# A soft mixture of experts behind windowed attention: k and v of a batch loaded in rows of 36 tokens on every other partition, and expert 6's w2 all in column slabs

## The chip, the cores and the metric

The kernel runs on one core of one Trainium2 chip. The metric is the time of one execution in device microseconds; lower is better. Four runs of the kernel before took 177.62 to 177.84 us, with a median of 177.7 us.

## The reference

The inputs are q, k and v of shape (8 batches, 8 heads, 576 tokens, 64) and the weights phi (512, 32), w1 (8, 512, 1024) and w2 (8, 1024, 512), all float32.

```
scores = q @ k.T / 8            # per batch and head
# heads 0-3: token i sees j with 0 <= i-j < 32
# heads 4-7: token i sees j with 0 <= i-j < 128 and (i-j) % 4 == 0
attn = softmax(where(mask, scores, -1e9)) @ v
x = attn as (4608 tokens, 512)
logits = x @ phi                                # 32 slots, 4 for each of 8 experts
slot_input = softmax(logits, over tokens).T @ x
slot_out[e] = relu(slot_input[e] @ w1[e]) @ w2[e]
out = softmax(logits, over slots) @ slot_out    # (4608, 512)
```

## The kernel before

**Tiling.** The attention is cut into 16 halves: half i is batch i // 2, with the first four heads (the plain window) if i is even and the last four (the window with steps of 4) if it is odd. `half(i)` (line 476) writes down all operations of a half. q, k and v of a half come from memory in three transfers (`load_half`, line 330), each with 128 rows: partition 32*h + p holds 18 consecutive tokens of head h, so a row is 18 x 64 values, 4608 bytes read and 2304 written, since the transfer turns float32 into bf16. The staging area has NSTG = 4 places, so it holds four halves. VectorE turns each staged tensor in blocks of 32 x 32 words (a word is a pair of bf16 values) into the layout that the matmuls read, with the pairs of the head dimension on partitions (`turn`, lines 485 to 497; one instruction of 576 words, or four short ones at line 494 for q of an odd half). The turned tensors stand in `o_kqv`, two places of one half each.

After that a half runs through scores with the mask added by a matmul (lines 509 to 533, TensorE), exponentials (548, ScalarE), v turned by TensorE and copied (570, 576), the product with v (603, 627), division by the row sum (610, 614, 635, 638, VectorE) and a turn of x (654 to 677). An odd half then adds the logits (693), their exponentials (701) and the slot inputs (730, 735, 743) of its batch.

**The experts.** All weights are kept in SBUF as bf16. w1 takes 2 MB of reading per expert and w2 as much. `w2off` (line 314) puts w2 of experts 0 to 4 into an area of their own and w2 of experts 5 to 7 over the staging area, so the loads of the latter have to wait until the last staged tensor has been turned (`rd` at lines 390 to 392). Most weights are loaded whole, in rows of 8192 written bytes (`w1_piece`, `w2_piece`). The last part of w2 comes in column slabs (`w2_slab`): first columns 0 to 255 of all remaining rows, then columns 256 to 511, in rows of 512 written bytes. Before the change the slabs hold the second half of expert 6's rows and all of expert 7's, 1.5 MB of reading for each slab, in pieces of 4, 4, 2, 1 and 1 rows for each partition; the first half of expert 6 is loaded whole, as a transfer of 4 rows for each partition.

**The end.** Behind the attention come the two layers of the experts (`L1` at 818, `L2` at 857), which read the weights in the order in which they land. When the first slab is in, columns 0 to 255 of the slot outputs are complete (881), and the output tiles of those columns are computed (901), scaled (910 on ScalarE, 913 on VectorE) and stored (922) for the first five half groups of tokens (NA = 2.5). When the second slab is in, the other columns of those, and then all other groups in whole rows, follow. The output is 9.4 MB in float32.

**What sets the order.** The kernel does not leave its order to a compiler. Each operation is written down with its engine, a duration that was put in by hand and a priority from `OFFS` and `PERIOD`; `Sched.run` (line 121) plays this through and gives each engine's order, and semaphore waits are added where an operation needs another engine's result. The loads of q, k, v and of all weights but one (half of expert 0's w1, on SyncE's queue) are issued by GpSimd on one queue, q0, in an order written out by hand: lines 779 to 786 put the three loads of half i, then `W_AFTER[i]` weight pieces, then those of half i + 1. A load that has to wait on GpSimd holds up all behind it. The stores are issued by SyncE on another queue.

Of the kernel before, what the change touches and what calls it, by code (L numbers as in the profile page):

```python
# [12 lines left out]
B, H, S, D = 8, 8, 576, 64  # L13
# [5 lines left out]
NH = 16  # L19


W_AFTER = [0, 1, 1, 0, 1, 0, 1, 0, 1, 0, 1, 0, 1, 0, 0, 99]
PERIOD = 22.6
NSTG = 4
PE_SLOW = 1.1
LRU = 130.0

OFFS = dict(T=64.4, SC=177.5, EX=-17.6, MK=58.6, TB=-42.6, VE=-89.4, PV=-21.2, RC=-6.8,
            NM=-229.1, XT=-20.7, XE=15.1, LG=-37.0, EXL=132.1, ET=25.9, EE=0.6, SI=26.7, SA=50.4)


class Buf:
# [164 lines left out]
def bass_dilated_sliding_attn__then__soft_moe_slots_kernel(  # L197
# [15 lines left out]
    def take(n):  # L213
        o = top[0]
        top[0] = o + (n + 1) // 2 * 2
        return o

    o_w1 = take(8 * 4 * FF)
    o_w2 = take(5 * 8 * DM)
    o_stg = take(max(NSTG * 3 * 1152, 3 * 8 * DM))  # L220
    o_kqv = [take(3 * 1152) for _ in range(2)]
    NP = 4
    PW = 4 * 320 + 64
    o_p = [take(PW) for _ in range(NP)]
# [33 lines left out]
    def a(off, dims, p0=0, pn=128):  # L258
        return AP(ar, p0 * NBF + off, [[NBF, pn]] + dims)
# [4 lines left out]
    def af(off, dims, p0=0, pn=128):  # L264
        return AP(ar_f.tensor, (p0 * NBF + off) // 2, [[NBF // 2, pn]] + dims)
# [22 lines left out]
    def dvet(n, psum=False):  # L288
# [1 line left out]

    b_id, b_mp, b_md, b_oh, b_sel, b_rm, b_phst, b_phis = (Buf(n) for n in
        ("id", "mp", "md", "oh", "sel", "rm", "phst", "phis"))
    b_stg = [[Buf(f"stg{i}{j}") for j in range(3)] for i in range(NSTG)]
    b_kqv = [[Buf(f"kqv{i}{j}") for j in range(3)] for i in range(2)]
    b_p = [Buf(f"p{i}") for i in range(NP)]
    b_vb = [[Buf(f"vb{i}{j}") for j in range(2)] for i in range(NVB)]
    b_xp = [Buf(f"xp{i}") for i in range(NX)]
# [8 lines left out]
    b_w1 = [Buf(f"w1{e}") for e in range(8)]  # L306
    b_w2 = [[Buf(f"w2{e}{s}") for s in range(2)] for e in range(8)]
    b_sx = Buf("sx")
    b_w6h = Buf("w6h")
    b_w2h = [[Buf(f"w2h{x}{s}") for s in range(2)] for x in range(4)]  # L310
    b_htz, b_rt, b_so = Buf("htz"), Buf("rt"), [Buf("soA"), Buf("soB")]
    b_hsb = [Buf(f"hsb{x}") for x in range(2)]
# [5 lines left out]
    def sem(n):  # L318
        return [nc.alloc_semaphore(n), 0]

    s_stg = [[sem(f"s_in{i}{j}") for j in range(3)] for i in range(NSTG)]
    loads = {}

    def dma_in(fn, nbytes, s, prio, name, **kw):
# [2 lines left out]
        loads[name] = o  # L327
        return o

    def load_half(i):  # L330
        b, dl = i // 2, i % 2
        s = i % NSTG
        for j, src in ((1, k), (0, q), (2, v)):
            def fn(src=src, j=j, s=s, b=b, dl=dl):
                return pool.dma_start(  # L335
                    a(o_stg + (s * 3 + j) * 1152, [[1, 1152]]),
                    src[b, 4 * dl:4 * dl + 4].rearrange("h (p t) d -> (h p) (t d)", p=32))
            dma_in(fn, 128 * 1152 * 4, s_stg[s][j], (-100.0 if i < 2 else -80.0) + i, f"ld{i}{'qkv'[j]}",
                   writes=[b_stg[s][j]])

    wq = []
    shared = {}
# [20 lines left out]
    def w2_piece(e, c0=0, n=8):  # L363
        def fn():
            return pool.dma_start(
                a(w2off(e) + c0 * DM, [[1, n * DM]]),
                moe_w2[e].rearrange("(p c) f -> p (c f)", c=8)[:, c0 * DM:(c0 + n) * DM])
        return (fn, n << 18, f"w2_{e}{c0}", b_w2[e] if e < 6 else [b_w6h])

    def w2_slab(e, s, c0=0, n=8):  # L370
        def fn():
            return pool.dma_start(  # L372
                a(w2off(e) + 256 * s + c0 * DM, [[DM, n], [1, 256]]),
                moe_w2[e].rearrange("(p c) f -> p c f", c=8)[:, c0:c0 + n, 256 * s:256 * s + 256])
        return (fn, n << 17, f"w2s_{e}{s}{c0}", [b_w2[e][s] if e == 6 else b_w2h[(0, 4, 6, 7).index(c0)][s]])

    wq += [w1_piece(e, 2 if e == 0 else 0) for e in range(8)]
    wq += [w2_piece(e) for e in range(6)] + [w2_piece(6, 0, 4)]
    for s in range(2):
        wq += [w2_slab(6, s, 4, 4), w2_slab(7, s, 0, 4), w2_slab(7, s, 4, 2),  # L380
               w2_slab(7, s, 6, 1), w2_slab(7, s, 7, 1)]
    nw = [0]

    def load_w(n):
        for _ in range(n):
            if nw[0] >= len(wq):
                return
            fn, nb, name, wr = wq[nw[0]]
            e = int(name.split("_")[1][0])
            rd = []  # L390
            if name.startswith("w2") and e >= 5:
                rd = [x for y in b_stg for x in y]
            nw[0] += 1
            dma_in(fn, nb, w_sem(name), rate=384e3 if name[2] == "s" else 422e3,
                   lag=(2.9 if name[2] == "s" else 2.3) if name[:2] == "w2" else 0.8, prio= -100.0 if nw[0] < 2 else -80.0, name=name, writes=list(wr) + rd)


    op(SP, lambda: spq.dma_start(
        af(w2off(4), [[1, 2048]]),
        w1_rows(0)[:, :2048]), .1, -200.0,  # L400
       kind="dma", nbytes=1 << 20, sem=sem("s_w1f"), writes=b_w2[4], name="w1f")
    for x in range(2):
        op(ACT, lambda x=x: act.activation(
            a(o_w1 + 1024 * x, [[1, 1024]]), af(w2off(4) + 2048 * x, [[1, 1024]]), ACTF.Copy),
            1.1, -200.0, reads=b_w2[4], writes=[b_w1[0]], name=f"w1c{x}")


    def const_ops():
# [67 lines left out]
    def half(i):  # L476
        b, dl = i // 2, i % 2
        T0 = i * PERIOD
        st, kq = i % NSTG, i % 2
        pr = lambda s: T0 + OFFS[s]  # L480
        ok, oq, ov = (o_kqv[kq] + 1152 * j for j in range(3))
        bq, bk, bv = b_kqv[kq][0], b_kqv[kq][1], b_kqv[kq][2]
        oq, ok = ok, oq

        def turn(j, o_dst):
            src = o_stg + (st * 3 + j) * 1152
            if not (dl and j == 0):
                return dve.transpose(au(o_dst, [[1, 18], [18, 32]]), au(src, [[32, 18], [1, 32]]))  # L488
            for x in range(4):

                na = (18 - x + 3) // 4
                t0, t1 = x, 18 + x
                at = [(t % 4) * 144 + t // 4 for t in (t0, t1)]
                last = dve.transpose(  # L494
                    au(o_dst + 2 * at[0], [[1, na], [9, 16], [at[1] - at[0], 2]]),
                    au(src + 64 * x, [[128, na], [1, 32]]))
            return last

        for j, o_dst in ((1, ok), (0, oq), (2, ov)):
            first_t.append(op(  # L500
                DVE, lambda j=j, o_dst=o_dst: turn(j, o_dst),
                1.43 if dl and j == 0 else 1.24, pr("T") + (0.5 if j == 2 else 0.0),
                reads=[b_stg[st][j]], writes=[b_kqv[kq][j]], name=f"T{i}{'qkv'[j]}"))

        def sc_fn(r):
            last = None
# [262 lines left out]

    last_ex = [None]  # L770
    for i in range(NH):
        load_half(i)
        half(i)
        if i == 0:
            load_phi(first_t[0])
        if i in (9, 13):
            row_sums(0 if i == 9 else 3, 3 if i == 9 else 6, 15 * PERIOD)
    names = [w[2] for w in wq]
    load_w(99)
    dma_order, w_at = [], 0  # L780
    for i in range(NH):
        dma_order += [f"ld{i}{c}" for c in "kqv"]
        dma_order += names[w_at:w_at + W_AFTER[i]]
        w_at += W_AFTER[i]
    for x, y in zip(dma_order, dma_order[1:]):
        loads[y].ord = loads[x]
    assert len(dma_order) == len(loads)
# [63 lines left out]
    def l2(es, x, col, n, cs=range(8), bufs=None):  # L851
        def fn():
            last = None
            for c in cs:
                for e in es:
                    g, j = e // 4, e % 4
                    last = pe.matmul(pf(sobank[x].idx, 0, [[1, n]], 32 * j, 32),  # L857
                                     a(o_htz + 1024 * g + 128 * c + 32 * j, [[1, 32]]),
                                     a(w2off(e) + DM * c + col, [[1, n]]),
                                     start=(c == 0 and g == 0 or x > 0 and c == (4 if e == 6 else 0)),  # L860
                                     stop=(c == (3 if e == 6 and x == 0 else 7) and (x > 0 or e in (3, 4, 5, 6))))
            return last

        op(PE, fn, pet(len(cs), n * .92), T1 + 5 + 2 * es[0] + (20 if x == 2 else 0) + cs[0] / 8,
           reads=[b_htz] + (bufs or [b_w2[e][y] for e in es for y in range(2)]),
           rmw=[sobank[x]], name=f"L2{es[0]}{x}{cs[0]}")

    l2((0, 1, 2, 3), 0, 0, 512)
    l2((4,), 0, 0, 512)
    l2((5,), 0, 0, 512)  # L870
    l2((6,), 0, 0, 512, range(4), [b_w6h])
    op(ACT, lambda: act.activation(a(o_so, [[1, 512]], 0, 64), pf(sobank[0].idx, 0, [[1, 512]], 0, 64),
                                   ACTF.Copy), actt(512), T1 + 10, reads=[sobank[0]], writes=b_so,
       name="SOx")
    op(DVE, lambda: dve.tensor_copy(af(o_sx, [[1, 512]], 64, 64), pf(sobank[0].idx, 0, [[1, 512]], 64, 64)),
       dvet(512, True), T1 + 10, reads=[sobank[0]], writes=[b_sx, b_p[2]], name="SOy")
    for x in (1, 2):
        l2((6,), x, 256 * x - 256, 256, range(4, 8), [b_w2[6][x - 1]])
        for y, cs in enumerate((range(4), range(4, 6), range(6, 7), range(7, 8))):
            l2((7,), x, 256 * x - 256, 256, cs, [b_w2h[y][x - 1]])  # L880
        op(DVE, lambda x=x: dve.tensor_tensor(  # L881
            a(o_so + 256 * x - 256, [[1, 256]], 64, 64), pf(sobank[x].idx, 0, [[1, 256]], 64, 64),
            af(o_sx + 512 * x - 512, [[1, 256]], 64, 64), AluOp.add), dvet(256, True),
           T1 + 10 + 20 * x, reads=[sobank[x], b_sx], writes=[b_so[x - 1]], name=f"SO{x - 1}")
# [139 lines left out]
```

## Time and profile before

| | |
|---|---|
| median of 4 runs | 177.7 us |
| the profiled execution | 177.78 us |
| its span in the profile | 176.0 us |
| TensorE, matmuls busy | 123.7 us (70% of the span) |
| VectorE busy | 121.0 us (69%) |
| ScalarE busy | 104.4 us (59%) |
| GpSimd busy | 44.6 us (25%) |
| read from memory, written to it | 61.93 MB, 9.44 MB, 406 GB/s over the span |

The page of the profile gives, after such totals, the span in 40 equal slices of 4.4 us. A digit there is the busy share of an engine in tenths; the row DMA is the mean busy share of the 16 DMA engines, and GB/s is what they moved, counted in written bytes. Then come the DMA queues with their packets and bytes (a packet is one row as one engine moves it), and the issues of transfers with the median time from issue to landing. A timeline lists instructions in order of time as start, duration, engine, line, operation and tiles; in brackets stands how long the engine was idle before and what ended that. PE is TensorE's matmuls, PEld its weight loads, DVE VectorE, ACT ScalarE, POOL GpSimd and SP SyncE. The profile's span is shorter than the time of the execution by 1.78 us.

### The profile page before, as it was taken

The page shows a single profiled execution, that of the slowest core. Times are in us where ns is not written, and L with a number is a line of the kernel's source. Part 1 is how long each engine was busy: PE and PEld are TensorE (multiplying, and loading weights), DVE is VectorE, ACT ScalarE, POOL GpSimd, SP SyncE. Part 2 cuts the span into 40 slices and gives each one's busy share as a digit, 9 for nine tenths or more (in the row PEclk, how much of TensorE's full clock was granted, in tenths as well). Part 3 has the DMA queues.
Part 4 walks back from the last instruction along what each step waited for, and adds up shares of the span by engine and source line. Part 5 has one row for each costly group of instructions (what it writes and reads, how often), then busy time and mean ns, then how long its engine had stood idle before and what let it go on. Part 6 is the DMA issues. An engine that isn't in the chain of part 4 may idle for free.

```text
span 176.0 us, 4779 instructions
## 1 busy us (share of the span) xinstructions
PE 123.7 (70%) x2098; PEld 83.5 (47%) x2098; DVE 121.0 (69%) x218; ACT 104.4 (59%) x165; POOL 44.6 (25%) x90
## 2 busy tenths in 40 slices
PE   0008767798899989889698889996776566897000
PEld 0005545676567667567477467775433123431000
DVE  6899589698988997995997899757220002699200
ACT  2404498697889789689489668884411001499000
POOL 7659632132412321420550000394000000000000
PEclk9999999999999999999999999999999999999655
DMA  5999999999999999999999999999999999999997
GB/s 171 243 210 210 221 204 214 219 208 208 219 211 208 222 208 209 221 210 204 216 216 210 207 216 219 216 214 220 212 216 216 209 194 189 281 330 413 419 425 318
DMA packets 16469, 41.26 MB, mean 234 GB/s; under 512 B 1729, under 2 KB 7361, under 8 KB 13889
## 3 DMA queue, kind: packets, MB, share of 16 engines
q0 software_dynamic: 12304, 30.41, 89.4%
q1 hardware_dynamic: 4144, 10.55, 15.9%
q8 instruction: 16, 0.26, 0.5%
q14 instruction: 5, 0.03, 0.0%
HBM read 61.93 MB, written 9.44 MB: 406 GB/s over the span
## 4 chain that ended last, share of the span: by engine, by line
DMA 47%; DVE 22%; PE 11%; ACT 6%; POOL 4%; issue 2%; POOLq 0%; DVEq 0%
DMA ar<-in_v_dram 29%; DMA ar<-in_moe_w_dram 18%; DVE ar L488 7%; DVE ar L913 6%; ACT ar L548 3%; PE ps L509 3%; POOL ar L372 3%; DVE ar L614 2%; PE ps L603 2%; DVE ar L444 2%; PE ps L570 1%; PE ps L516 1%; DVE ar L449 1%; DVE ar L494 1%; ACT ar L670 1%
## 5 line engine op out<-in xcount | busy, mean ns | idle before, releaser
L488 DVE STREAM_TRANSPOSE ar<-ar 128x576 uint32<-128x576 uint32 x40 | 48.8, 1242 | 5.2 <-DMA ar<-in_k_dram 3.7
L548 ACT ACTIVATE ar<-ps 128x1152 bf16<-128x1152 f32 (+1 forms) x32 | 38.0, 1186 | 24.2 <-PE ps L533 15.0
L509 PE MATMUL ps<-ar 128*128 128x320 bf16 (+1 forms) x128 | 22.7, 301 | 18.2 <-DVE ar L488 13.7
L614 DVE TENSOR_TENSOR ar<-ps,fs 96x768 bf16<-96x768 f32 (+1 forms) x32 | 26.3, 822 | 1.2
L576 ACT ACTIVATE ar<-ps 128x768 bf16<-128x768 bf16 x32 | 25.0, 812 | 1.1 <-PE ps L570 1.0
L509 PEld LDWEIGHTS ps<-ar 128*128 128x128 bf16 x128 | 10.4, 99 | 23.2 <-DVE ar L488 13.7
L603 PE MATMUL ps<-ar 128*128 128x65 bf16 x320 | 14.7, 193 | 4.5 <-ACT ar L548 3.9
L570 PE MATMUL ps<-ar 128*128 128x128 bf16 x192 | 15.8, 228 | 1.9 <-DVE ar L614 1.0
L335 POOL DMA_DIRECT2D ar<-in_k_dram x16 | 8.8, 553 | 28.1 <-DVE ar L488 25.0
L603 PEld LDWEIGHTS ps<-ar 128*128 128x128 bf16 x320 | 12.0, 97 | 7.5 <-ACT ar L548 4.5
L910 ACT ACTIVATE ar<-ps,fs 128x512 f32<-128x512 f32 (+1 forms) x23 | 11.4, 638 | 5.7 <-PE ps L901 5.7
L857 PE MATMUL ps<-ar 128*32 128x512 bf16 (+1 forms) x76 | 10.8, 347 | 5.3 <-DMA ar<-in_moe_w_dram 4.6
L570 PEld LDWEIGHTS ps<-ar 128*128 128x128 bf16 x192 | 12.4, 118 | 3.2 <-DVE ar L614 1.5
L913 DVE TENSOR_SCALAR ar<-ps,fs 128x512 f32<-128x512 f32 (+1 forms) x23 | 12.7, 625 | 1.0 <-PE ps L901 1.0
L335 POOL DMA_DIRECT2D ar<-in_v_dram x16 | 8.8, 547 | 13.6 <-DVE ar L488 10.3
L610 DVE RECIPROCAL fs<-ps 96x12 f32<-96x12 f32 (+1 forms) x32 | 6.5, 202 | 7.7 <-PE ps L603 7.2
L901 PE MATMUL ps<-ar 128*128 128x512 bf16 (+1 forms) x46 | 9.9, 340 | 1.3 <-DVE ar L881 1.0
L335 POOL DMA_DIRECT2D ar<-in_q_dram x16 | 8.7, 544 | 7.9 <-DVE fs L610 4.2
L670 ACT ACTIVATE ar<-ps 128x576 bf16<-128x576 bf16 x16 | 9.7, 659 | 0.9 <-PE ps L654 0.7
L693 PE MATMUL ps<-ar 128*128 128x288 bf16 x64 | 9.2, 287 | 1.2 <-ACT ar L677 1.2
L857 PEld LDWEIGHTS ps<-ar 128*32 128x32 bf16 x76 | 4.5, 96 | 11.6 <-DMA ar<-in_moe_w_dram 8.4
L673 ACT ACTIVATE ar<-ps 128x1024 bf16<-128x1024 bf16 x8 | 8.2, 1030 | 2.5 <-PE ps L660 2.3
(75 smaller groups left out, 181.1 us busy)
## 6 DMA issues: line engine op xcount, KB each, us to landing
ar<-in_moe_w_dram POOLq DMA_DIRECT2D x13, 1024.0 KB, 28.2
out_dram<-ar SPq DMA_DIRECT2D x6, 1024.0 KB, 8.6
ar<-in_k_dram POOLq DMA_DIRECT2D x16, 288.0 KB, 22.7
ar<-in_q_dram POOLq DMA_DIRECT2D x16, 288.0 KB, 23.3
ar<-in_v_dram POOLq DMA_DIRECT2D x16, 288.0 KB, 22.9
out_dram<-ar SPq DMA_DIRECT2D x10, 256.0 KB, 3.1
ar<-in_moe_w_dram SPq DMA_DIRECT2D x1, 1024.0 KB, 5.1
ar<-in_moe_w_dram POOLq DMA_DIRECT2D x2, 512.0 KB, 21.4
```

The lines of the kernel that those rows point to most:

```text
L335: return pool.dma_start(a(o_stg + (s * 3 + j) * 1152, [[1, 1152]]), src[b, 4 * dl:4 * dl + 4].rearrange("h (p t) d -> (h p) (t d)", p=32))
L488: return dve.transpose(au(o_dst, [[1, 18], [18, 32]]), au(src, [[32, 18], [1, 32]]))
L509: pe.matmul(pf(h, 0, [[1, W]]), a(o_id, [[1, 128]]), a(msk, [[1, W]]), start=True, stop=False)
L548: eo = op(ACT, lambda P=P, W=W: act.activation(a(P, [[W, 4], [1, W]]), AP(ps, 0, [[4096, 128], [512, 4], [1, W]]), ACTF.Exp, scale=SCALE), ...
L570: last = pe.transpose(pb(bank.idx, bb * 256 + par * 32, [[64, 4], [1, 32]]), src, a(o_id, [[1, 128]]))
L576: op(ACT, lambda t=t, bank=bank: act.activation(a(o_vb[vs] + 3 * t * VBK, [[66, 12], [2, 32], [1, 2]]), pb(bank.idx, 0, [[64, 12], [1, 32] ...
L603: last = pe.matmul(pf(bank.idx + x, 65 * t, [[1, 65]]), w, a(VB + t * VBK + 66 * h, [[1, 65]]), start=True, stop=True)
L614: op(DVE, lambda hp=hp, bank=bank: dve.tensor_tensor(a(ox + 128 * hp, [[64, 2], [256, NT], [1, 64]], 0, rows), pf(bank.idx, 0, [[512, 2], ...
L670: fn = lambda c=c + x, bank=bank: act.activation(a(o_xt[xt] + 576 * c, [[1, 576]]), pb(bank.idx, 0, [[1, 576]]), ACTF.Copy)
L857: last = pe.matmul(pf(sobank[x].idx, 0, [[1, n]], 32 * j, 32), a(o_htz + 1024 * g + 128 * c + 32 * j, [[1, 32]]), a(w2off(e) + DM * c + co ...
L910: op(ACT, lambda: act.activation(dst, src(), ACTF.Copy, scale=sca), actt(cw, .1), prio + .1, reads=[bank, b_rinv], writes=wr, name=f"OE{G} ...
L913: op(DVE, lambda: dve.tensor_scalar(dst, src(), sca, None, op0=AluOp.mult), dvet(cw, True) + .08, prio + .1, reads=[bank, b_rinv], writes= ...
```

## The change

Three things are changed together, and the planner's priorities (`OFFS`, `PERIOD`) are other numbers.

For batches 1 to 7, k and v are loaded in rows of 36 tokens. One transfer takes four heads: 64 rows of 9216 bytes read and 4608 written. The first four heads go to the even partitions, the last four to the odd ones. A block of 32 partitions then holds one head of the first four and one of the last four, and two VectorE instructions for each tensor turn the whole batch, for both halves together. q, and all of batch 0, are loaded and turned as before. The staging area holds NSTG = 2 batches in place of four halves, with the same bytes; a k or v load waits until both instructions that turn this tensor of the batch two before are done. The turned tensors need twice the room: one of the two places is put over w2 of expert 3 and a part of expert 4's, whose loads now wait for the last use of what stands there.

The weights between the batches are one piece fewer: six w1 pieces come before the last batch's loads, and seven did. The first megabyte of expert 0's w1 is staged in the place of expert 0's w2, where it was expert 4's.

The half of expert 6's w2 rows that was loaded whole goes back into the slabs, which so hold all of experts 6 and 7, 2 MB of reading each. Expert 5's w2 is loaded in two halves of 4 rows for each partition in place of one transfer, and each half has matmuls of its own.

```diff
-W_AFTER = [0, 1, 1, 0, 1, 0, 1, 0, 1, 0, 1, 0, 1, 0, 0, 99]
-PERIOD = 22.6
-NSTG = 4
+W_AFTER = [1, 0, 1, 1, 1, 1, 1, 99]
+PERIOD = 8.7
+NSTG = 2
+LOADS = (((1, 0), (0, 0), (2, 0), (1, 1), (0, 1), (2, 1)), ((1, 0), (1, 1), (0, 0), (2, 0), (2, 1), (0, 1)))
...
-    o_stg = take(max(NSTG * 3 * 1152, 3 * 8 * DM))
-    o_kqv = [take(3 * 1152) for _ in range(2)]
+    o_stg = take(max(NSTG * 3 * 2304, 3 * 8 * DM))
+    o_kqv = [o_w2 + 3 * 8 * DM, take(3 * 2304)]
...
+    def load_batch(b):
+        s = b % NSTG
+        for j, x in LOADS[b > 0]:
+            def fn(j=j, x=x, src=(q, k, v)[j][b, 4 * x:4 * x + 4]):
+                o = o_stg + (s * 3 + j) * 2304
+                if j == 0 or b == 0:
+                    return pool.dma_start(a(o + 1152 * x, [[1, 1152]]),
+                                          src.rearrange("h (p t) d -> (h p) (t d)", p=32))
+                return pool.dma_start(AP(ar, x * NBF + o, [[2 * NBF, 64], [1, 2304]]),
+                                      src.rearrange("h (u t) d -> (h u) (t d)", u=16))
+            dma_in(fn, 128 * 1152 * 4, s_stg[s][j][x], (-100.0 if b < 1 else -80.0) + 2 * b,
+                   f"ld{b}{'qkv'[j]}{x}", writes=[b_stg[s][j][x]] if j == 0 or b == 0 else b_stg[s][j])
...
-    wq += [w2_piece(e) for e in range(6)] + [w2_piece(6, 0, 4)]
+    wq += [w2_piece(e) for e in range(5)] + [w2_piece(5, 0, 4), w2_piece(5, 4, 4)]
     for s in range(2):
-        wq += [w2_slab(6, s, 4, 4), w2_slab(7, s, 0, 4), w2_slab(7, s, 4, 2),
+        wq += [w2_slab(6, s), w2_slab(7, s, 0, 4), w2_slab(7, s, 4, 2),
                w2_slab(7, s, 6, 1), w2_slab(7, s, 7, 1)]
...
+        def turn(j, x):
+            src = o_stg + (st * 3 + j) * 2304
+            return dve.transpose(au(o_kqv[kq] + 2304 * j + 36 * x, [[1, 18], [36, 16], [576, 2]]),
+                                 au(src + 64 * 18 * x, [[32, 18], [1, 32]]))
...
+        for j in (1, 0, 2):
+            if j == 0 or b == 0:
+                first_t.append(op(
+                    DVE, lambda j=j: turn_half(j), 1.43 if dl and j == 0 else 1.24,
...
+            elif not dl:
+                for x in range(2):
+                    op(DVE, lambda j=j, x=x: turn(j, x), 1.24, pr("TK" if j == 1 else "TV") + .05 * x,
+                       reads=b_stg[st][j], writes=b_kqv[kq][j], name=f"T{b}{'qkv'[j]}{x}")
...
-    l2((5,), 0, 0, 512)
-    l2((6,), 0, 0, 512, range(4), [b_w6h])
+    for y in range(2):
+        l2((5,), 0, 0, 512, range(4 * y, 4 * y + 4), [b_w5h[y]])
...
     for x in (1, 2):
-        l2((6,), x, 256 * x - 256, 256, range(4, 8), [b_w2[6][x - 1]])
+        l2((6,), x, 256 * x - 256, 256, bufs=[b_w2[6][x - 1]])
```

## The prediction

> **What bounds the kernel now.** I read the 40 slices first, then the queues, then stretches of the DMA record, and last the weight loads of TensorE at the end.
>
> ```profile
> PE   0008767798899989889698889996776566897000
> DVE  6899589698988997995997899757220002699200
> DMA  5999999999999999999999999999999999999997
> GB/s 171 243 210 210 221 204 214 219 208 208 219 211 208 222 208 209 221 210 204 216 216 210 207 216 219 216 214 220 212 216 216 209 194 189 281 330 413 419 425 318
> q0 software_dynamic: 12304, 30.41, 89.4%
> ```
>
> No compute engine is full over the span, and DVE is nearly idle after slice 28. The DMA row is 9 from the second slice to the last but one. GB/s counts what is written: on q0 each bf16 byte written is two fp32 bytes read, so 210 there is 420 read. The transfers set the end; anything that does not change how long the 16 DMA engines need, or when the last load is in, is free.
>
> ```profile
> ar<-in_k_dram POOLq DMA_DIRECT2D x16, 288.0 KB, 22.7
> ar<-in_q_dram POOLq DMA_DIRECT2D x16, 288.0 KB, 23.3
> ar<-in_v_dram POOLq DMA_DIRECT2D x16, 288.0 KB, 22.9
> ```
>
> A q, k or v load lands 23 us after its issue in the median, though one takes about 1.4 us: the queue has some 20 us of work in front of each. That is the cover for every wait on POOL.
>
> Now the price of a row. Each stretch below holds q0 packets of one size: 2304 B (q, k, v) from 94 to 104 us, 8192 B (whole weight rows) from 108 to 138, 512 B (column slabs) from 144.5 to 148.5. The packets under 512 B are the completion marks, one per engine and transfer.
>
> ```profile
> DMA packets 1014, 2.11 MB, mean 211 GB/s; under 512 B 112, under 2 KB 112, under 8 KB 1012
> q0 software_dynamic: 1012, 2.07, 109.8%
> ...
> q0 software_dynamic: 878, 6.41, 102.4%
> ...
> DMA packets 1594, 0.78 MB, mean 194 GB/s; under 512 B 79, under 2 KB 1594, under 8 KB 1594
> q0 software_dynamic: 1594, 0.78, 144.6%
> ```
>
> One packet of one engine therefore takes 10 us x 16 / (1012 - 112) = 177.8 ns at 2304 B; 30 us x 16 / (878 - 96) = 613.8 ns at 8192 B (96 marks there); 4 us x 16 / (1594 - 79) = 42.2 ns at 512 B. A line through the outer two is 4.1 ns per packet plus 0.0744 ns per byte. It gives 175.6 ns at 2304 B, 2.2 below the measured, and 347.1 ns at 4608 B. Packets overlap (the shares are over 100%), so the mean duration of one record (192 ns at 2304 B, 60 ns at 512 B) is not its price: those would give a fixed 22 ns per packet, five times too much.
>
> Last, the loads of the column stage, each seen by the matmuls that wait for it:
>
> ```profile
> 141.51 1.41 PEld L857 LDWEIGHTS ps<-ar 128*32 128x32 bf16 x8 [3.34 <-DMA ar<-in_moe_w_dram]
> 143.96 0.54 PEld L857 LDWEIGHTS ps<-ar 128*32 128x32 bf16 x4 [1.05 <-DMA ar<-in_moe_w_dram]
> 145.31 0.33 PEld L857 LDWEIGHTS ps<-ar 128*32 128x32 bf16 x4 [0.80 <-DMA ar<-in_moe_w_dram]
> 146.69 0.33 PEld L857 LDWEIGHTS ps<-ar 128*32 128x32 bf16 x4 [1.06 <-DMA ar<-in_moe_w_dram]
> 147.33 0.11 PEld L857 LDWEIGHTS ps<-ar 128*32 128x32 bf16 x2 [0.31 <-DMA ar<-in_moe_w_dram]
> 147.68 0.09 PEld L857 LDWEIGHTS ps<-ar 128*32 128x32 bf16 x1 [0.24 <-DMA ar<-in_moe_w_dram]
> 148.02 0.09 PEld L857 LDWEIGHTS ps<-ar 128*32 128x32 bf16 x1 [0.25 <-DMA ar<-in_moe_w_dram]
> ...
> 151.37 0.11 PEld L857 LDWEIGHTS ps<-ar 128*32 128x32 bf16 x2 [0.34 <-DMA ar<-in_moe_w_dram]
> 151.72 0.09 PEld L857 LDWEIGHTS ps<-ar 128*32 128x32 bf16 x1 [0.24 <-DMA ar<-in_moe_w_dram]
> 152.16 0.09 PEld L857 LDWEIGHTS ps<-ar 128*32 128x32 bf16 x1 [0.34 <-DMA ar<-in_moe_w_dram]
> ```
>
> Expert 5 is in at 141.51, the whole half of expert 6 2.45 us later, then two half-MB slab pieces after 1.35 and 1.38 us. The last load is in at 152.16; from there to the end of the span are 23.8 us, nearly all of it stores at the DMA rate. So the end is **the last landing plus 23.8 us**.
>
> **The change, part by part.** The sum is made against the profiled execution: 177.78 us, a span of 176.0 and 1.78 around it, 0.08 over the median of the runs, 177.70.
>
> 1. *Longer rows.* For batches 1 to 7, k and v come in 7 x 4 = 28 transfers of 64 rows of 4608 B (written) in place of 28 of 128 rows of 2304 B. Bytes and number of transfers stay. Each engine has 28 x 8 = 224 packets of 2304 B fewer and 112 of 4608 B more. One fixed cost goes per pair: 112 x 4.1 ns = **-0.46 us**. Bounds: nothing, if what is fixed belongs to the transfer and not to the packet; -1.15 us, if the long row runs at the per-byte rate of the 8192 B rows (613.8 x 4608 / 8192 = 345.3 ns against 2 x 177.8). I take the line, since 4608 lies inside it.
> 2. *Half of expert 6 back in slabs.* The 1 MB that landed in 2.45 us becomes two more half-MB pieces: 2 x 32 packets per engine x 42.2 ns = 2.70 us: **+0.25 us**. By the landings (1.35, 1.38) it is +0.25 to +0.31.
> 3. *Expert 5 in two halves.* 2 x 2.45 against 8 x 613.8 ns = 4.91 us: between -0.01 and +0.05 by whether a transfer has a cost of its own; **+0.03**.
> 4. *One w1 piece moves behind the last batch.* The same bytes on the same queue: 0. The last batch is in one piece earlier (4.9 us, so at about 102.6, from 107.5 by the record of landings), which gives attention more time.
> 5. *Transposes.* k and v of a batch take two DVE instructions of 576 words each, as before two halves did; q stays. 40 instructions of 1242 ns and 8 x 4 short ones before and after: 0. The output steps 36 words where it stepped 18; the short ones of L494 step 9 and a jump and take 1.17 us for as many words against 1.24, so a step costs nothing that can be seen.
> 6. *New waits on POOL.* A k or v load of batch b+2 waits for both transposes of that tensor of batch b, and everything behind it in POOL's written order waits too, weights included; the DMA queue is who would starve. The ring holds two batches, as many bytes as four halves did, so the 20 us of cover stay: 0, and microsecond for microsecond beyond. Expert 3's and 4's w2 now wait for the last matmuls on batch 6's k, q and v: the last exponentials of that batch start at 103.1 us, and expert 3's turn on the queue comes five weight pieces of 4.9 us after the last batch has landed, at about 102.6 + 24.5 = 127. Expert 5's w2 waits for the last transpose as it did (over at 112.6 us now, turn at about 137).
> 7. *The tail.* Slab 2 is 2 MB, not 1.5, so slab 1 lands 1.35 us earlier before the end of loads, and the stores of its columns start that much earlier. They fill idle engines, but the end hangs on the last landing, and they don't bring that forward: 0. If stores took turns with load packets, they would delay it. The second slab's last two pieces, with stores under way from 150.7, took 0.35 and 0.44 us; the first slab's, with none, 0.35 and 0.34. So at most 0.1 us now.
>
> L2's first group ended its work 2.85 us before expert 5 was in, and the tail matmuls are short: a compute path later by under 3 us costs nothing.
>
> Sum: -0.46 + 0.25 + 0.03 = -0.18: 177.6 profiled, **177.5** as a median. Ends of the known terms: -1.15 + 0.24 = -0.9 and 0 + 0.36 = +0.4.
>
> No row of this trace has 64 partitions. [...]
>
> **The rivals.**
> - *Forecast, 0.38:* the terms above, 177.5, own range 177.2 to 177.9.
> - *The whole gap between row lengths closes, 0.25:* -1.15 + 0.28 = -0.87, 176.8; from -0.64 in part 1 on it counts as faster. For: 2304 B rows lie 2.2 ns above the line. Against: part of those are the two instruction fetches in that stretch.
> - *Rows on every other partition run slower, 0.27:* a transfer of 64 rows writes in another partition order, and two engines may meet at one place of SBUF. Place: the 28 loads, 28 x 8 x 177.8 ns = 39.8 us. Each 1% is 0.40 us; from 1.4% it is slower than before by over 0.2%. Bounds: 0, and +40 if half of the engines stood idle. The nearest row of a transfer below its engines' rate is that of the half-row stores of slice 34 (330 GB/s against 419 of the whole-row stores of slice 37), a fifth; I take a twentieth, nearer to nothing, since all three row sizes of q0 lie within 2.2 ns of one line: +2.0, 179.5. For: nothing here has run this shape. Against: q0 writes half of what it reads, so a write side has room.
> - *Stores take turns with slab 2, 0.05:* the extra 1.35 us of slab doubles: 178.9. Against: the 0.1 us of part 7.
> - *The ring runs dry, 0.03:* waits on the whole batch use up the 20 us of cover; each gap counts whole, a gap of 1 us makes 178.5. Against: part 6.
> - *The transfer uses half of the engines, 0.02:* it doesn't do what it says; +40, 217.
>
> **How the numbers follow.** 0.2% is 0.36 us and about what a measurement of this kernel can tell from no change. The forecast's 0.38 splits into 0.07 faster, 0.28 same, 0.03 slower; the partition rival leaves 0.04 within. Faster 0.07 + 0.25 = 0.32; same 0.28 + 0.04 = 0.32; slower 0.03 + 0.23 + 0.05 + 0.03 + 0.02 = 0.36. The range takes in the faster rival with 0.1 to spare and the slower ones but the last and half of the next: 176.7 to 179.5.
>
> **What would show it.** Right: packets of 4608 B at about 347 ns in a stretch of k and v; the last landing at 152.0; the distance from it to the end still 23.8 us; no fall of GB/s between slices 2 and 30. Wrong: a GB/s row lower in the middle (partitions), a slice under 9 in the DMA row (dry ring), small pieces of slab 2 over 0.4 us apart (stores), or TensorE's L857 not waiting for loads.

## The result, and the profile after

The changed kernel takes 177.53 us (median of 34 runs, 177.36 to 177.85) against 177.71 (52 runs): a ratio of 0.9990, 95% interval 0.9985 to 0.9994, or -0.18 us with 0.09 on either side. That is faster beyond chance, and less than 0.2%. Below, a difference is a difference of such ratios times 177.7 us, since every run has its own runs of the kernel before on the same chip beside it. Of the four runs of e11 below, the profiled one was a slow one (183.8 us), so its +2.5 us comes from the three fast ones and no time is read from its profile.

The profiled execution of the changed kernel took 177.85 us, the longest of its runs, with a span of 176.07 us; so the two spans don't show the gain. In this execution TensorE's granted clock was 0.50 from 145.7 to 152.5 us, where it was 1.00 in the kernel before, so its matmuls there are not to be compared one to one. From its page:

```profile
DVE  6899359998998998998698898349220014399200
DMA  5999999999999999999999999999999999989997
GB/s 179 237 210 215 212 214 210 220 208 210 219 212 211 223 207 211 224 205 211 221 208 211 219 216 216 216 210 223 214 214 207 203 195 183 306 300 416 422 419 315
q0 software_dynamic: 11536, 30.41, 88.7%
...
ar<-in_k_dram POOLq DMA_DIRECT2D x16, 288.0 KB, 13.6
ar<-in_q_dram POOLq DMA_DIRECT2D x16, 288.0 KB, 15.5
ar<-in_v_dram POOLq DMA_DIRECT2D x16, 288.0 KB, 15.2
```

The bytes of q0 are the same in 768 packets fewer: 1792 from the long rows, less 896 and 128 for the slabs' and expert 5's. GB/s is even up to slice 32, so the queue never ran dry (slices are counted from 1). Two things are new. The DMA row has an 8 in slice 36, where it had 9, and GB/s falls from 306 to 300 there, where it rose from 281 to 330. And loads land 14 to 15 us after their issue, not 23. The weight loads of TensorE at the end:

```profile
141.36 0.54 PEld L876 LDWEIGHTS ps<-ar 128*32 128x32 bf16 x4 [2.05 <-DMA ar<-in_moe_w_dram]
143.88 0.77 PEld L876 LDWEIGHTS ps<-ar 128*32 128x32 bf16 x8 [1.98 <-DMA ar<-in_moe_w_dram]
145.23 0.33 PEld L876 LDWEIGHTS ps<-ar 128*32 128x32 bf16 x4 [0.59 <-DMA ar<-in_moe_w_dram]
145.88 0.13 PEld L876 LDWEIGHTS ps<-ar 128*32 128x32 bf16 x2 [0.32 <-DMA ar<-in_moe_w_dram]
146.24 0.10 PEld L876 LDWEIGHTS ps<-ar 128*32 128x32 bf16 x1 [0.23 <-DMA ar<-in_moe_w_dram]
146.59 0.10 PEld L876 LDWEIGHTS ps<-ar 128*32 128x32 bf16 x1 [0.25 <-DMA ar<-in_moe_w_dram]
...
152.00 0.10 PEld L876 LDWEIGHTS ps<-ar 128*32 128x32 bf16 x1 [0.21 <-DMA ar<-in_moe_w_dram]
```

The last load is in at 152.00 us, against 152.16: 0.16 us earlier, where the sum has 0.18. One execution each can't settle so little: the runs e7, e10 and e12 below, with the same loads in the same order, have it at 151.72, 151.88 and 151.83. The landing records can. Each transfer has one record from each of the 16 DMA engines; the mean of the 16 depends less on the slowest of them. By these means, from the last load of batch 0 to the last load of all take 136.60 us in the changed kernel and 136.80 in the kernel before, and 136.58 to 136.64 in e4, e7, e10 and e12. So the loads are 0.20 us shorter. The first slab is in at 146.59, 1.43 us earlier than it was.

### The profile page after: what moved, and what is told of

Same layout as the page of the kernel before. It is cut to its first block, busy times and chain, and to the rows that moved or that the text cites. A ratio compares the mean times of both kernels' runs of the same rounds, so it can differ in the third digit from the quotient of the medians.

```text
span 176.1 us, 4785 instructions
## 1 busy us (share of the span) xinstructions
PE 127.2 (72%) x2102; PEld 85.9 (49%) x2102; DVE 120.4 (68%) x218; ACT 105.2 (60%) x165; POOL 44.8 (25%) x90
## 4 chain that ended last, share of the span: by engine, by line
DMA 31%; PE 26%; DVE 25%; ACT 5%; issue 3%; POOL 2%; DVEq 0%
DMA ar<-in_moe_w_dram 20%; DMA ar<-in_v_dram 12%; PE ps L527 6%; DVE ar L495 6%; DVE ar L932 6%; PE ps L588 3%; ACT ar L566 3%; PE ps L876 3%; DVE ar L501 2%; DVE ar L632 2%; PE ps L534 2%; PE ps L711 2%; PE ps L621 2%; PE ps L544 2%; DVE ar L452 2%
## 5 line engine op out<-in xcount | busy, mean ns | idle before, releaser
L527 PE MATMUL ps<-ar 128*128 128x320 bf16 (+1 forms) x128 | 23.4, 308 | 16.0 <-DVE ar L501 13.8
L495 DVE STREAM_TRANSPOSE ar<-ar 128x576 uint32<-128x576 uint32 x28 | 33.2, 1237 | 0.6 <-DMA ar<-in_v_dram 0.6
L527 PEld LDWEIGHTS ps<-ar 128*128 128x128 bf16 x128 | 10.8, 101 | 21.1 <-POOL ar L425 13.7
L621 PE MATMUL ps<-ar 128*128 128x65 bf16 x320 | 15.3, 195 | 4.3 <-ACT ar L566 2.0
L588 PE MATMUL ps<-ar 128*128 128x128 bf16 x192 | 16.4, 234 | 1.6 <-DVE ar L632 1.3
L621 PEld LDWEIGHTS ps<-ar 128*128 128x128 bf16 x320 | 12.2, 98 | 7.8 <-ACT ar L566 2.8
L501 DVE STREAM_TRANSPOSE ar<-ar 128x576 uint32<-128x576 uint32 x12 | 14.6, 1242 | 1.5 <-DMA ar<-in_q_dram 1.5
L343 POOL DMA_DIRECT2D ar<-in_k_dram x14 | 7.5, 541 | 31.1 <-DVE ar L495 17.4
L588 PEld LDWEIGHTS ps<-ar 128*128 128x128 bf16 x192 | 13.1, 119 | 3.0 <-DVE ar L632 1.5
L628 DVE RECIPROCAL fs<-ps 96x12 f32<-96x12 f32 (+1 forms) x32 | 6.5, 202 | 10.9 <-PE ps L621 10.5
L876 PE MATMUL ps<-ar 128*32 128x512 bf16 (+1 forms) x80 | 10.6, 373 | 3.9 <-DMA ar<-in_moe_w_dram 3.3
L920 PE MATMUL ps<-ar 128*128 128x512 bf16 (+1 forms) x46 | 11.0, 371 | 1.3 <-DVE ar L900 1.0
L372 POOL DMA_DIRECT2D ar<-in_moe_w_dram x7 | 3.8, 552 | 23.6 <-PE ps L551 21.8
L507 DVE STREAM_TRANSPOSE ar<-ar 128x160 uint32<-128x160 uint32 (+1 forms) x32 | 9.7, 414 | 0.0
```

The source lines that it names most:

```text
L495: return dve.transpose(au(o_kqv[kq] + 2304 * j + 36 * x, [[1, 18], [36, 16], [576, 2]]), au(src + 64 * 18 * x, [[32, 18], [1, 32]]))
L501: return dve.transpose(au(dst, [[1, 18], [18, 32]]), au(src, [[32, 18], [1, 32]]))
L527: pe.matmul(pf(h, 0, [[1, W]]), a(o_id, [[1, 128]]), a(msk, [[1, W]]), start=True, stop=False)
L588: last = pe.transpose(pb(bank.idx, bb * 256 + par * 32, [[64, 4], [1, 32]]), src, a(o_id, [[1, 128]]))
L621: last = pe.matmul(pf(bank.idx + x, 65 * t, [[1, 65]]), w, a(VB + t * VBK + 66 * h, [[1, 65]]), start=True, stop=True)
```

## The experiments

**Theory A** is the prediction's: the DMA queue is full to the last load, so the time moves by packets (a fixed cost each) and bytes, and the end is the last landing plus the stores. **Rival B:** the slabs' length pays or costs by when the stores start. **Rival C:** what changed on k and v comes from the partitions or the order, not from the packets. **Theory D** was formed on the way and is told there. Each difference in the last column is good to about 0.2 us either way (an estimate, from the two ratios' intervals added in quadrature), and to 0.4 to 0.7 us in e5, e6 and e8.

| run | median, us | ratio to before, 95% | against the changed kernel |
|---|---|---|---|
| changed kernel | 177.53 | 0.9990 (0.9985 to 0.9994) | |
| e1 short slabs | 177.31 | 0.9974 (0.9964 to 0.9983) | -0.28 |
| e2 before, long slabs | 177.90 | 1.0012 (1.0003 to 1.0021) | +0.21 against before |
| e3 rows cut in two | 178.04 | 1.0016 (1.0007 to 1.0025) | +0.46 |
| e4 neighbouring partitions | 177.53 | 0.9989 (0.9980 to 0.9998) | 0.0 |
| e5 q in long rows | 187.21 | 1.0541 (1.0501 to 1.0582) | +9.8 |
| e6 seven pieces first | 179.03 | 1.0080 (1.0060 to 1.0101) | +1.6 |
| e7 nine half groups | 177.44 | 0.9989 (0.9981 to 0.9998) | 0.0 |
| e8 slabs of expert 7 | 187.20 | 1.0550 (1.0527 to 1.0573) | +10.0 |
| e9 short slabs, six half groups | 177.27 | 0.9980 (0.9971 to 0.9989) | -0.18 |
| e10 six half groups | 177.09 | 0.9971 (0.9960 to 0.9981) | -0.34 |
| e11 before, six pieces first | 180.19 | 1.0140 (1.0125 to 1.0156) | +2.5 against before |
| e12 four half groups | 177.91 | 1.0011 (1.0001 to 1.0021) | +0.37 |

### The terms of the sum, one at a time

Short slabs in the changed kernel:

```diff
-    wq += [w2_piece(e) for e in range(5)] + [w2_piece(5, 0, 4), w2_piece(5, 4, 4)]
+    wq += [w2_piece(e) for e in range(6)] + [w2_piece(6, 0, 4)]
...
-        wq += [w2_slab(6, s), w2_slab(7, s, 0, 4), w2_slab(7, s, 4, 2),
+        wq += [w2_slab(6, s, 4, 4), w2_slab(7, s, 0, 4), w2_slab(7, s, 4, 2),
```

> The changed kernel with the column stage of the kernel before: expert 5's w2 whole, half of expert 6's w2 rows whole, slabs of 1.5 MB. Theory A (fixed cost per packet on a full DMA queue): the two terms of the tail, +0.25 and +0.03 us, are taken back: 177.53 - 0.28 = 177.25 us, the last landing 0.28 us earlier. Rival B (longer slabs pay for themselves, since the stores of the first columns start earlier against the end of the loads): the same as the changed kernel or slower, 177.5 to 178.

Measured: -0.28 us, as A has it; the last load is in at 151.61. Rival B falls. The same edit the other way round, in the kernel before:

> The kernel before with the column stage of the changed kernel: expert 5's w2 in two halves, slabs of 2 MB, everything else as before. Theory A: 177.71 + 0.28 = 177.99 us, the last landing 0.28 us later. Rival B: 177.7 or less.

Measured: +0.21 us. The last landing did not move as expected: its profile, of one of its fastest executions, has it at 152.12 us, against 152.16. By the means over the 16 engines, the part from the last load of batch 7 to the last load of all takes 50.11 us in the changed kernel and 49.89 with short slabs, 44.94 in the kernel before (which loads one weight piece fewer there) and 45.19 with long ones. So the two terms of the tail, put at 0.28 us, measure 0.23 and 0.24.

The rows of k and v cut in two:

```diff
-                return pool.dma_start(AP(ar, x * NBF + o, [[2 * NBF, 64], [1, 2304]]),
-                                      src.rearrange("h (u t) d -> (h u) (t d)", u=16))
+                return pool.dma_start(AP(ar, x * NBF + o, [[2 * NBF, 64], [1168, 2], [1, 1152]]),
+                                      src.rearrange("h (u a t) d -> (h u) a (t d)", u=16, a=2))
...
-                                 au(src + 64 * 18 * x, [[32, 18], [1, 32]]))
+                                 au(src + 1168 * x, [[32, 18], [1, 32]]))
```

> The changed kernel, but each k and v row of 36 tokens is written as two pieces of 18 tokens with a gap of 32 bytes between them, so that the packets have 2304 bytes again; partitions, order, number of transfers and bytes stay. Theory A: 112 pairs per engine get their fixed 4.1 ns back, 177.53 + 0.46 = 178.0 us. Rival C (what was gained or lost on k and v comes from the partitions or the new order, not from the packets): 177.5 us, and a load still takes what it took with long rows.

Measured: +0.46 us, last load at 152.36. Partitions, transposes, waits and order are the changed kernel's; the packets are shorter, and the pieces lie 32 bytes apart. Rival C falls. 112 pairs per engine make **4.1 ns for a packet**, and 2.5 to 5.7 by the error of 0.2 us. The landing means are finer: from the last load of batch 0 to the last of batch 7 takes 86.93 us here and 86.46 to 86.53 in the changed kernel, e4, e7, e10 and e12, which makes 3.6 to 4.2 ns. That is the fixed cost that the prediction read off three row sizes of the trace.

The two groups of heads on neighbouring partitions:

```diff
-                return pool.dma_start(AP(ar, x * NBF + o, [[2 * NBF, 64], [1, 2304]]),
+                return pool.dma_start(AP(ar, 64 * x * NBF + o, [[NBF, 64], [1, 2304]]),
```

> The changed kernel, but the k and v rows of the first four heads of batches 1 to 7 go to partitions 0 to 63 and those of the last four to 64 to 127, in place of even and odd ones; the transposes are left as they are, so from batch 1 on heads and tokens are mixed up and the output is not the reference's, while every instruction and byte stays. [...] Own view, from the records of this case: q0 writes half the bytes that it reads, so half of the places can still take them: 177.5 to 179 us. If the DMA engines too were halved, 217 us.

Measured: no difference. So 64 rows cost nothing here, on every other partition or on neighbouring ones, and no rival about partitions is left. From 94 to 99 us the queues moved 212 GB/s in written bytes in this run, 211 in the changed kernel and 208 in the kernel before, with its rows on 128 partitions. That half of the places can still take the writes was the author's view; no run shows such places. These transfers turn float32 into bf16, and what loads that write as much as they read would do on 64 partitions was not tested.

### Pushing the idea on: a new bound

q in long rows as well, on top of short slabs:

```diff
-                if j == 0 or b == 0:
+                if b == 0:
...
-                                a(oq + 288 * res + par, [[2, 128]], 32 * h, 32),
+                                a(oq + 2 * res + par, [[8, 128]], 32 * h, 32),
```

> The changed kernel with the column stage of the kernel before (as in the run with short slabs, 177.31 us) and q of batches 1 to 7 loaded and turned like k and v, in rows of 36 tokens; odd halves read q in token order with a step in place of the order by residue. Theory A (fixed cost per packet): 14 more transfers, 14 x 4 = 56 pairs per engine x 4.1 ns = 0.23 us less: 177.08 us. Rival (the gain of the long rows is spent, or the stepped reads of q make the matmuls of odd halves so slow that attention ends late): 177.3 or more.

Measured: 187.21 us. The one instruction that turns two halves leaves q of an odd half in token order, so its matmuls read q with a step of 16 bytes. The score matmuls of the odd halves, first in the changed kernel, then here (groups by line and shape: count, busy, mean ns):

```profile
L544 PE MATMUL ps<-ar 32*128 32x128 bf16 x256 | 7.6, 235 | 0.0
```

```profile
L534 PE MATMUL ps<-ar 32*128 32x128 bf16 x256 | 18.2, 412 | 0.0
```

That is 10.6 us more of TensorE's time; the matmuls of 64 columns beside them take 2.2 us less (4.0 against 6.2). Attention closes late: L810 here is L820 of the changed kernel, which starts at 129.3 us, and L910 computes the first output tiles.

```profile
146.25 0.30 PE L810 MATMUL ps<-ar 32*128 32x32 bf16 x4 [0.77 <-DVE ar L751]
...
158.56 1.53 PE L910 MATMUL ps<-ar 128*128 128x256 bf16 x10
```

Attention is over 17 us later, and the stores start at 159.6 us, 10.9 later. How much of the 17 us the slow matmuls make by themselves was not tested: the order of the loads within a batch, the transposes and the engines' orders changed too. The DMA row of the run, and its GB/s:

```profile
DMA  6999999999999999999999999999999950499997
GB/s 191 225 212 214 215 210 216 218 208 222 212 206 220 213 210 220 211 209 225 207 211 223 212 216 217 214 203 214 214 216 195 194 68 4 131 342 403 422 415 322
```

The hole in slices 33 to 35 (148 to 162 us) is not a load queue run dry. By the landing records the last load was in at 151.52 us; from there on the DMA engines had next to nothing to move until the first store (4 GB/s in slice 34). A wait on POOL for the place that w2 of expert 3 shares (28.7 us) left a dent at most: 180 and 188 GB/s from 124 to 126 us, and 203 in slice 27 (121 to 125 us), which has 214 on either side. So the short rows of q bought a layout that TensorE reads faster (235 against 412 ns). The run with slabs of expert 7 alone was built on this one and says nothing of its own question:

```diff
-    wq += [w2_piece(e) for e in range(6)] + [w2_piece(6, 0, 4)]
+    wq += [w2_piece(e) for e in range(6)] + [w2_piece(6, 0, 4), w2_piece(6, 4, 4)]
...
-        wq += [w2_slab(6, s, 4, 4), w2_slab(7, s, 0, 4), w2_slab(7, s, 4, 2),
+        wq += [w2_slab(7, s, 0, 4), w2_slab(7, s, 4, 2),
```

> The previous idea with q in long rows, and all of expert 6's w2 loaded whole in two halves, so that the slabs hold expert 7 alone, 1 MB each. Theory A: one more MB at 2.45 us in place of 2.70, -0.25 us against the run with q in long rows: 176.8 us; the first stores come 2.65 us after the first slab, and the second slab takes 2.7 us, so the slowest engine still goes from load to store without a gap. Rival B (short slabs leave the engines without work before the first stores): 177.1 or more.

Measured: 187.20 us. The last load landed at 151.01 us, 0.5 before that of the run it was built on, but here the stores don't wait for it. Whether slabs of 1 MB would do was left open.

### The place of one weight piece

> The changed kernel with one weight piece after batch 1 too, so that seven w1 pieces come before the last batch's loads, as in the kernel before. Theory A (only the work of the queue counts, its order not): 177.53 us. Rival (a part of the gain comes from the last batch landing one piece earlier): up to 177.7 or more, with matmuls of the second layer late.

```diff
-W_AFTER = [1, 0, 1, 1, 1, 1, 1, 99]
+W_AFTER = [1, 1, 1, 1, 1, 1, 1, 99]
```

Measured: +1.6 us, so A's 177.53 was wrong. The last landing did not move (151.86 us by the landing records, 151.95 in the changed kernel); attention did. Matmuls of the changed kernel, then of this run:

```profile
129.29 0.31 PE L820 MATMUL ps<-ar 32*128 32x32 bf16 x4 [0.77 <-DVE ar L761]
...
147.51 2.32 PE L920 MATMUL ps<-ar 128*128 128x256 bf16 x10 [0.52 <-DVE ar L900]
```

```profile
134.30 0.30 PE L820 MATMUL ps<-ar 32*128 32x32 bf16 x4 [0.77 <-DVE ar L761]
...
140.69 6.08 PE L876 MATMUL ps<-ar 128*32 128x512 bf16 x64 [0.54 <-DVE ar L861]
149.19 1.05 PE L876 MATMUL ps<-ar 128*32 128x256 bf16 x8 [2.42 <-DMA ar<-in_moe_w_dram]
150.18 1.53 PE L920 MATMUL ps<-ar 128*128 128x256 bf16 x10
```

L820 closes attention: 129.3 us, and 5.0 later with the piece before the last batch. The planner then puts matmuls on the second slab, which has to land first, ahead of the first output tiles (L920): 147.5 becomes 150.2, and the stores start late. The mirror image in the kernel before:

```diff
-W_AFTER = [0, 1, 1, 0, 1, 0, 1, 0, 1, 0, 1, 0, 1, 0, 0, 99]
+W_AFTER = [0, 1, 0, 0, 1, 0, 1, 0, 1, 0, 1, 0, 1, 0, 0, 99]
```

> The kernel before with one weight piece fewer before the last batch (none after the third half), so that the last batch lands 4.9 us earlier and the same bytes follow, as in the change. Theory A (the place of the piece costs and brings nothing by itself): 177.7 us, the slot-input transpose that ends attention no later than 128.7 us. Rival (the gain of the change is that earlier landing): 177.5 us or less.

Measured: +2.5 us; A and its rival both missed. With the last batch loaded one piece earlier, this kernel was slower. Both runs move more than the queue: the planner's times, and so the orders of all engines, come from the same list, with priorities chosen for another one. They show that the list and the priorities hang together, and not what the place alone is worth.

### The stores: theory D

> The changed kernel with NA = 4.5: nine half groups, not five, are stored by column halves, so there are 0.26 MB x 4 more stores to run beside the second slab. Theory A (the load queue is not slowed by the stores; the end is the last landing plus the stores): the last landing stays at 152.0 us of the span; four half groups of 0.52 MB in rows of 1 KB at some 350 GB/s in place of 8 KB at 419 cost 0.25 us each, 177.53 + 1.0 = 178.5 us. Rival (stores take turns with loads): the last landing moves to 153 or later, the total to 179 or more.

```diff
-    NA = 2.5
+    NA = 4.5
```

Measured: no difference, and the last load in at 151.72. So the stores don't delay the last load, but A's +1.0 us was wrong too. Where it went is seen in single microseconds: first the kernel before, then the changed kernel (busy time of each engine, granted clock, DMA share, GB/s):

```profile
153.00:154.00 1.00, 1.00 (x10) 0.93 (x10) 0.59 (x2) 0.70 (x2) 0.00 (x0) 1.00 1.06 364
154.00:155.00 1.00, 1.00 (x7) 0.52 (x5) 1.00 (x4) 1.00 (x4) 0.00 (x0) 1.00 0.79 278
```

```profile
153.00:154.00 1.00, 0.99 (x9) 0.92 (x10) 0.54 (x2) 0.66 (x2) 0.00 (x0) 1.00 0.78 273
154.00:155.00 1.00, 1.00 (x7) 0.56 (x5) 1.00 (x3) 1.00 (x4) 0.00 (x0) 1.00 0.42 149
```

The changed kernel issues its first store at 148.7 us, the kernel before at 149.8; five half groups are stored before the second slab's columns are computed, and the queue of stores has a hole. The low granted clock ahead of it in this one execution is not the cause: e4, with the same stores and a granted clock of 1.00 from 149 to 157 us, has it too, with 454 GB/s in the two microseconds together against 422 here and 642 before.

```profile
153.00:154.00 1.00, 0.95 (x9) 0.80 (x8) 0.89 (x3) 1.00 (x3) 0.00 (x0) 1.00 0.57 200
154.00:155.00 1.00, 0.87 (x4) 0.49 (x5) 1.00 (x3) 1.00 (x4) 0.00 (x0) 1.00 0.75 254
```

More first stores fill it and cost 0.25 us each for their short rows (the estimate in the expectation of e7). That is theory D; one more, and one fewer (the loop over the rest of the half groups starts later or earlier to match):

```diff
-    NA = 2.5
+    NA = 3
```

> The changed kernel (slabs of 2 MB) with NA = 3 as its one edit. Theory A: 177.53 + 0.25 = 177.8 us. Theory D: its faster engines are idle for longer than with short slabs (from the end of the fifth store at 153.7 to the landing of the next ones at 155.9 in its record, of which a store takes 0.75), so the whole 0.74 - 0.25 = 0.5 us is won: 177.05 us.

```diff
-    NA = 2.5
+    NA = 2
```

> The changed kernel with NA = 2: four half groups by column halves, one fewer. Theory A (last landing plus stores priced by their rows): 0.25 us less, 177.28 us. Theory D (the queue of stores runs empty between the columns): the hole that the changed kernel shows from 153 to 155 us grows by one store, 0.74 us, and 0.25 are saved: 177.53 + 0.5 = 178.0 us, with less than 149 GB/s in the microsecond from 154 on.

Measured: -0.34 us (177.09) and +0.37 us (177.91). A has the sign wrong in both. The same two microseconds with six, then with four half groups:

```profile
153.00:154.00 1.00, 1.00 (x10) 0.80 (x8) 0.86 (x3) 0.97 (x3) 0.00 (x0) 1.00 1.07 367
154.00:155.00 1.00, 1.00 (x5) 0.52 (x6) 1.00 (x4) 1.00 (x4) 0.00 (x0) 1.00 0.85 291
```

```profile
153.00:154.00 1.00, 0.95 (x9) 0.77 (x7) 0.92 (x3) 1.00 (x3) 0.00 (x0) 1.00 0.50 177
154.00:155.00 1.00, 1.00 (x6) 0.49 (x5) 1.00 (x3) 1.00 (x4) 0.00 (x0) 1.00 0.48 156
```

One number of D's missed: with four, 154 on was to be under 149 GB/s, and the hole opened a microsecond earlier instead, at 259 GB/s from 152 to 153. In the three profiles the distance from the last load to the end goes the same way: 23.3 us with six, 24.1 with five, 24.3 with four. With short slabs (the diff of e1, and `NA = 3`) there is little to fill:

> The changed kernel with short slabs (177.31 us) and NA = 3: six half groups stored by column halves, in place of five. Theory A (the end is the last landing plus the stores, each priced by its rows): 0.25 us for one more half group in 1 KB rows, 177.31 + 0.25 = 177.56 us. Theory D (formed after the run with nine half groups cost nothing: between the last store of the first columns and the first of the second the faster engines stand idle for about 1 us, and more first stores fill that): the first store of the second columns comes 3.35 us after the last landing as before, 0.74 us of stores of those left to do then are already done, one more half group costs 0.25: 177.31 - 0.74 + 0.25 = 176.8 us if the faster engines set the end, 177.0 if the slowest one does.

Measured: -0.18 us against the changed kernel, +0.1 against the run with five half groups, within the error. D's 176.8 to 177.0 missed; A's 177.56, or +0.25, can't be told from +0.1. By the landing records the fastest engine's hole with five was 0.26 us, not 1 us, so one more store about paid for itself. The lowest time is that of the changed kernel with six half groups, 177.09 us; short slabs with five take 177.31, and by their ratios (0.9971 and 0.9974) the two can't be told apart. The two gains don't add up.

## Why the prediction was right

The forecast, 177.5 us and a move of -0.18, was met (177.53, -0.18). The mechanism was right: the loads take 0.20 us less, and the way from the last load to the end, 23.8 us before, is 23.9 in e3 and e4, which store as the changed kernel does. That time and forecast agree to a hundredth is luck, since the measurement is good to 0.09 us and part 1 alone had bounds of 0 and -1.15. Term by term:

- *Part 1, longer rows, -0.46:* the cut rows give it back, +0.46 in the time and 0.40 to 0.47 in the landing means. The rival "whole gap closes" (-0.87) and the zero end fall. No long stretch of the trace holds rows of 4608 bytes alone, so their 347 ns were not read directly.
- *Parts 2 and 3, slabs and halves, +0.28 together:* -0.28 and +0.21 in the time from the two sides, 0.23 and 0.24 in the landing means. The split between the two was not measured.
- *Part 4, the moved piece, 0:* right as far as the last landing goes, which stayed within 0.1 us when it was moved back. But "gives attention more time" was no gift: in the changed kernel attention closes at 129.3 us, 0.6 later than before (128.7), with the last batch in 5.5 us earlier (101.9 us by the landing records, 107.4 before). The cost that this hides is in no term of the sum. Whether the whole-batch loads or the plan cause it was not settled.
- *Part 5, transposes, 0:* 28 and 12 whole instructions of 1237 and 1242 ns, and the same short ones. Right.
- *Part 6, waits on POOL, 0:* the sum right, a reason wrong. The cover did not stay at 20 us; the median fell to 14 to 15. It was enough, and nearly so even in the run with slow matmuls, whose last load was in at 151.5 us.
- *Part 7, the tail, 0:* the stores indeed left the loads alone: the last two pieces of slab 2 landed 0.35 and 0.38 us after the ones before. The 8 in slice 36 of the DMA row, by the prediction the sign of a dry ring, lies behind the last load. But "the end is the last landing plus 23.8 us" is half of the rule. It holds for five half groups (24.1 in the profile of the changed kernel with its low clock, 23.9 in e3 and e4), because the stores' 1.1 us of lead turned into the hole that makes this 8; with one more half group 0.34 us of it were to be had.
- *The partition rivals (0.27 and 0.02):* refuted, even for neighbouring partitions (0.0 us in e4). No run shows engines that meet at one place of SBUF, or a transfer of 64 rows on half of the engines: the landing records of the changed kernel hold 16 landings for each transfer, and its DMA row is 9 from slice 2 to 35. The price of the first leaned on a row misread: the 330 GB/s stand in slice 36, not 34, and include the microsecond from 154 to 155 us with 278 GB/s, when the stores had a gap; the half-row stores beside it ran at 338 to 349.

The sum's numbers were met in e1 to e3, which change the loads alone, and missed in all runs from e5 on but e9, where it can't be told. They failed at the same point: the sum counted the DMA queue alone, where TensorE and the planner, beyond a slack of some 3 us, or an idle store queue set the end. The new priorities and the new place of the first megabyte of w1 were not tested by themselves.

## What to carry to other kernels

When the DMA queue is full, price a row by counting packets in a stretch of one row size, and not by a record's duration: records overlap (here they added up to 102 to 145% of the 16 engines' time). A last landing sets the end only if the stores behind it have no hole (filling it took 0.34 us off in e10); look at single microseconds there, and match the number of early stores to the length of the last load (with slabs of 2 MB six half groups beat five, with 1.5 MB the two can't be told apart). A written load order and tuned priorities are one thing: move one without the other and the plan may lose more than the edit is worth (1.6 us in e6, 2.5 in e11).

## What the runs showed of the hardware

- With a step of 16 bytes in the moving operand, in place of 4, a matmul of 32 rows and 128 columns took 412 ns (e5), where it takes 235 in the changed kernel. The mean granted clock of that run was lower too (0.92 against 0.95), but matmuls of 128 rows and 288 columns went only from 305 to 327 ns.
- Stores on one queue did not slow loads queued before on another: in the changed kernel the last two pieces of slab 2, with stores under way, landed 0.35 and 0.38 us after the ones before, and those of slab 1, with none, 0.36 and 0.35. In the kernel before, the last of the 16 landings of the first store came 0.66 us after that of the last load (152.78 and 152.12 us), and those of the next three stores, as large (16 packets of 1 KB for each engine), 0.68 to 0.70 us apart. So the slowest engine seems to have done the store after the load, though the first packet of that store had begun at 150.70 us, 1.1 before the last load packet ended (151.77).
- The 16 engines finish the last load 2.9 us apart (149.25 to 152.12 us in the kernel before, 149.07 to 151.95 in the changed one); after the first transfers they were 0.6 to 0.7 us apart. The records of each hold 16 instruction fetches of 16 KB, each of 0.89 to 0.98 us on one engine, and in the kernel before the distance grows in steps near some of these (at 23, 31, 81 and 97 us), not near all. That they are the cause was read from the records and not tested.
